# An attention, feed-forward and mixture-of-experts kernel on one core: the decay table is built through DRAM, and the first feed-forward units and the weight conversion move forward

## The chip, the cores and the metric

The kernel runs on one NeuronCore of a Trainium2 chip. The metric is device time in microseconds (us) of one execution. TensorE is called PE in the profile, VectorE DVE, ScalarE ACT, GpSimd POOL, and SyncE, which here only issues transfers, SP.

## The reference

Three layers follow one another on 1536 tokens of width 512. The first is linear attention with a decay per head, in blocks, with a running state per batch:

```
Dmask = where(rel >= 0, lam ** rel, 0)                       # per head
intra = ((q_block @ k_block.T) * Dmask) @ v_block
inter = (q_block * lam ** (pos + 1)) @ kv_state
out_block = intra + inter
kv_state = lam ** block * kv_state + (k_block * lam ** (block - 1 - pos)).T @ v_block
```

The second is a dense feed-forward layer, whose weights arrive as float64 bit patterns:

```
h = x @ w_in            # 512 x 2048
x = maximum(0.01 * h, h) @ w_out
```

The third picks one of eight experts per token by a gate and applies `relu(x @ w1[e]) @ w2[e]`, scaled by the gate.

## The kernel before

Each engine runs its instructions in the order in which the code writes them (a manual schedule); the order of the work is set by hand.

**Attention.** The 12 chunks of 128 tokens (`ORD`) are called 0 to 11. For a chunk, `at_scores` makes the scores on PE (tile `sc`), `at_mask` multiplies them on DVE by the decay table `dec` (tile `dec_t`, 128 x 8 heads x 128, result `pm`), `at_out` multiplies by `v` on PE (tile `ao`) and splits the result into a high and a low half for the next layer (`xh` on ACT, `xl` on DVE). `at_prep_q` multiplies queries by powers of the decay (`lq`, on POOL), `at_prep_k` the keys (on ACT for the chunks in `PREP_ACT`, else on POOL), `at_state` makes a chunk's contribution to the state on PE (tile `as`), and `at_state_add` puts it into the state (a copy on ACT for the first chunk of a batch, an addition on DVE after that). Chunks 0 and 1 are the first of the two batches.

**The decay table.** `make_dec` builds on DVE, in 8 rows of 256 numbers (`pw`, one row per head), zeros followed by the powers of lam. Line p of the table of head h is row h read from element p on. `load_dec` fetches it, before, by eight transfers out of `pw` in SBUF, one per head.

**Feed-forward.** Tokens are taken two chunks at a time (j = 0 to 5) and the hidden width in 16 slices f, so that there are 96 units u = 16 j + f. `ff1` makes 12 matmuls into `hp` and a scaled copy `t` on ACT, `ff1_max` the maximum on DVE, `ff1_split` the halves `gh` (ACT) and `gl` (DVE), and `ff2` six matmuls into `x`, `LAG` = 2 steps behind. The list `seq` gives the unit of each step i: 0, 1, 2, 16, 3, 17 and so on, so that from step 2 on each weight slice serves two units in turn. Attention work of later chunks hangs on the units as hooks (`at(j, f, ...)` runs behind unit 16 j + f).

**Weights.** Slice f has a tile `wi` and a tile `wo` (512 KB each as it arrives in `rawi`, `rawo`). Converting one takes four DVE instructions (three on bits at lines 1481 and 1486, one subtraction at line 1493) and one rounding on ACT (line 1491); `conv` does the same at lines 180 to 198 ahead of the loop. The table `todo` says which tiles a step converts: two in each of steps 0 to 2, one in each of steps 3 to 26. All loads go through SP's queue in the order of the code.

The lines to follow are `load_dec` (113), the mask (314), the split of the attention output (354, 355), the maximum (411) and the two lists at the end, `todo` and the hooks.

Of the kernel before, what the change touches and what calls it, by code (L numbers as in the profile page):

```python
# [18 lines left out]
B, H, S, D = 2, 8, 768, 64  # L19
NT, DM, DFF = 1536, 512, 2048  # L20
E, FE = 8, 1024
C = 128
# [4 lines left out]
NSTAT = 10  # L27
NPLAIN = 12
NAR = 32
PREP_ACT = (0, 1)  # L30
KV = {1: 'wo15', 2: 'wi15', 3: 'wo14'}
QK = {2: 'wi14', 3: 'wo13'}
NPOS = {2: 0, 3: 1, 4: 2}
# [7 lines left out]
def tile_attention_ffn_moe(  # L41
# [51 lines left out]
    def make_dec():  # L93
        nc.vector.memset(pw[:, 0:127], 0.0)
        nc.vector.memset(pw[:, 127:128], 1.0)
        nc.vector.tensor_copy(out=pw[:, 128:129], in_=lam_sb)
        m = 1
        while m < 128:
            nc.vector.tensor_scalar(
                out=pw[:, 128 + m:128 + 2 * m],  # L100
                in0=pw[:, 128:128 + m],
                scalar1=pw[:, 127 + m:128 + m],
                scalar2=None,
                op0=ALU.mult,
            )
            m *= 2

    def load_dec():

        base = pw[:, :]  # L110
        step = base.ap[0][0]
        for h in range(H):
            nc.sync.dma_start(
                out=dec[:, h, :],
                in_=bass.AP(tensor=base.tensor, offset=base.offset + h * step, ap=[[step, 1], [1, 128], [1, C]]),
            )

    def load_lq():
        nc.sync.dma_start(out=pw_d, in_=pw)
        base = pw_d[:, :]  # L120
        for half in range(2):
            nc.sync.dma_start(
                out=lq[half * 64:half * 64 + 64],
                in_=bass.AP(
                    tensor=base.tensor,
                    offset=base.offset + half * 256 + 128,
                    ap=[[0, 64], [512, H // 2], [1, C]],
                ),
            )
# [4 lines left out]
    def load_chunk(n, names):  # L134
        b, c = ORD[n]
        t = chunks.setdefault(n, {})
        for nm in names:
            if nm == "k" and c + 1 >= NCH:
                continue
            src = {"qT": qT, "kT": kT, "v": v, "k": k}[nm]  # L140
            if n in KV and nm in ("v", "k"):
                if "kv" not in t:
                    t["kv"] = wp.tile([128, 2, 512], F32, tag=KV[n], name="kv")
                t[nm] = t["kv"][:, int(nm == "k"), :]
            elif n in QK and nm in ("qT", "kT"):
                if "qk" not in t:
                    t["qk"] = wp.tile([128, 2, 512], F32, tag=QK[n], name="qk")
                t[nm] = t["qk"][:, int(nm == "kT"), :]
            else:
                t[nm] = qkv_p.tile([128, 512], F32, tag=nm, name=nm, bufs=2 if nm in ("qT", "kT") else 1)  # L150
            nc.sync.dma_start(out=t[nm], in_=src[b, c])
            if nm in ("qT", "kT"):
                t[nm] = t[nm].rearrange("p (g i) -> p g i", g=4)
            else:
                t[nm] = t[nm].rearrange("p (h d) -> p h d", h=H)
# [3 lines left out]
    def load_win(f):  # L159
        r = wp.tile([128, 4, 256], I32, tag=f"wi{f}", name=f"rawi{f}")  # L160
        nc.sync.dma_start(out=r.rearrange("p k f -> p (k f)"), in_=w_in[f])
        raw["wi", f] = r

    def load_wout(f):
        r = wp.tile([128, 1024], I32, tag=f"wo{f}", name=f"rawo{f}")
        nc.sync.dma_start(out=r, in_=w_out[f * 128:(f + 1) * 128, :])
        raw["wo", f] = r
# [93 lines left out]
    def warm_pe(n):  # L261
        wb = bank(0, "warm")
        for _ in range(n):
            nc.tensor.matmul(wb, lhsT=junk[:, 0:128], rhs=junk, start=True, stop=True)
# [9 lines left out]
    def at_prep_q(n):  # L274
        b, c = ORD[n]
        t = chunks[n]
        if c > 0:
            nc.gpsimd.tensor_mul(out=t["qT"], in0=t["qT"], in1=lq)  # L278
# [130 lines left out]
    def ff1_max(u):  # L409
        t, hp = gt[u]  # L410
        nc.vector.tensor_max(out=t, in0=t, in1=hp)  # L411
# [874 lines left out]
    def conv(tag, f, dst, eng):  # L1286
        split64_out(*split64([(tag, f, dst, eng)]))
# [2 lines left out]
    V, P = nc.vector, nc.gpsimd  # L1290
    nc.sync.dma_start(out=lam_sb, in_=lam.rearrange("(h o) -> h o", o=1))
    load_chunk(0, ("qT", "kT"))
    load_chunk(1, ("qT", "kT"))
    load_win(0)
    make_dec()
    load_dec()
    load_chunk(0, ("v",))
    load_chunk(1, ("v",))
    load_wout(0)
    load_chunk(0, ("k",))  # L1300
    load_chunk(1, ("k",))
    load_win(1)
    load_chunk(2, ("qT", "kT"))
    load_lq()
    load_chunk(3, ("qT", "kT"))
    load_wout(1)
    load_chunk(2, ("v", "k"))
    load_win(2)
    load_chunk(3, ("v", "k"))
    load_wout(2)  # L1310
    load_win(3)
    load_wout(3)
    load_win(4)
    load_wout(4)
    nc.scalar.copy(out=lam_sb2, in_=lam_sb)

    nc.gpsimd.memset(junk, 0.0)
    warm_pe(10)
    at_scores(0, 2, 7)
    conv("wi", 0, win, V)  # L1320
    at_scores(1, 5, 6)
    at_mask(0)
    at_mask_tw(1)
# [1 line left out]
    at_out(1, 4)  # L1325
    at_prep_k(0)
    at_prep_k(1)
    at_state(0, 2)
    at_state(1, 7)
    at_state_add(0)  # L1330
    at_state_add(1)
    conv("wo", 0, wout, V)

    NU = 16 * NCH
    last = NCH - 1
# [2 lines left out]
    def at(j, f, fn, *args):  # L1338
        hooks.setdefault(16 * j + f, []).append((fn, args))

    at(0, 0, at_out, 2, 2)
    at(0, 0, at_out, 3, 7)
    at(0, 1, at_state, 2, 3)
    at(0, 1, at_state, 3, 4)
    at(0, 1, at_state_add, 2)
    at(0, 1, at_state_add, 3)
    for f in range(11):
        at(0, f + 2, load_win, f + 5)
        at(0, f + 2, load_wout, f + 5)
# [112 lines left out]
            seq.append(16 + f - SKEW)  # L1462
    seq += range(32, NU)
    items = [(tag, f) for f in range(16) for tag in ("wi", "wo")]
    todo = {0: items[2:4], 1: items[4:6], 2: items[6:8]}
    for i in range(3, 27):
        todo[i] = items[i + 5:i + 6]
    late_sub = []

    def bits(job, n):  # L1470
# [21 lines left out]
        (win if tag == "wi" else wout)[f] = hl  # L1492
        late_sub.append(lambda: V.tensor_sub(out=hl[:, 1], in0=job[4].bitcast(F32), in1=hl[:, 0].bitcast(F32)))

    at_scores(2, 3, 4)
    at_prep_q(2)
    at_mask(2)
    at_scores(3, 5, 6)
    at_prep_q(3)
    at_mask(3)  # L1500
    at_prep_k(2)
    at_prep_k(3)
    for i in range(NU + LAG):
        u = seq[i] if i < NU else None
        if u is not None:
            ff1(u, i % 2)
            jobs = [[tag, f] for tag, f in todo.get(i, ())]
            for job in jobs:
                bits(job, 0)
            ff1_max(u)  # L1510
            for job in jobs:
                bits(job, 1)
            for fn in late_sub:
                fn()
            late_sub.clear()
            for job in jobs:
                bits(job, 2)
            ff1_split(u)
            for job in jobs:
                round_hi(job)  # L1520
            if i < 2:
                for fn in late_sub:
                    fn()
                late_sub.clear()
        if i >= LAG:
            w = seq[i - LAG]
            if w == NU - 1:
                G1(0, 0, 0, 7)
            ff2(w)
            if w % 16 == 15 and w // 16 not in (1, 2):  # L1530
                evac_x2(w // 16)
        for fn, args in hooks.get(u, ()):
            fn(*args)
# [156 lines left out]
```

## Time and profile before

| what | value |
|---|---|
| median of 3 runs | 546.64 us (545.68 to 546.86) |
| profiled execution | 545.67 us, its span in the trace 543.8 us |
| PE busy in the span | 498.4 us, 92% |
| DVE busy | 318.9 us, 59% |
| ACT busy | 174.4 us, 32% |
| POOL busy | 105.8 us, 19% |
| moved by DMA | 63.42 MB, mean 117 GB/s |

The profile follows one execution. The span is the time from the first to the last instruction of the trace; the 1.9 us between it and the execution's time lie around it. Times in rows count from the span's start. A busy share is a mean over stages that are limited by different things, so the stretch at the start is read by itself.

### The profile page before, as it was taken

How to read it: one execution, taken by the hardware profiler on the slowest of the kernel's cores; microseconds unless marked ns; L12 is line 12 of the kernel's file. 1: busy time of each engine (PE TensorE's matmuls, PEld its weight loads, DVE VectorE, ACT ScalarE, POOL GpSimd, SP SyncE). 2: the span in 40 equal slices, each digit the busy share in tenths (PEclk: the TensorE clock that was granted, in tenths of full speed). 3: DMA queues.
4: the chain of work that ended last, by engine and by line, in shares of the span. 5: the costliest groups of instructions: out<-in, count | busy, mean ns of one | idle time of the engine just before them, and what ended most of it. 6: DMA issues, size and time to landing. Idle time of an engine off the chain costs nothing. (4 is left out here: it accounts for less than half of the span.)

```text
span 543.8 us, 9414 instructions
## 1 busy us (share of the span) xinstructions
PE 498.4 (92%) x3488; PEld 424.1 (78%) x3488; DVE 318.9 (59%) x767; ACT 174.4 (32%) x409; POOL 105.8 (19%) x142
## 2 busy tenths in 40 slices
PE   4078799998999999999999999899999999999994
PEld 2067698787788888887898898787789997969693
DVE  3137989999867777768366737874652141613130
ACT  1052343333442223322232224544332253422221
POOL 1004001103202120102102106334031212232111
PEclk9577899999999999999999999999999999999998
DMA  6779950080090110310040007221049717365101
GB/s 131 91 250 410 401 209 1 0 288 1 9 303 4 40 41 0 108 41 29 0 156 2 21 1 235 75 61 57 4 137 382 265 39 264 131 200 196 40 2 41
DMA packets 30764, 63.42 MB, mean 117 GB/s; under 512 B 6967, under 2 KB 8895, under 8 KB 30704
## 3 DMA queue, kind: packets, MB, share of 16 engines
q1 hardware_dynamic: 28592, 56.17, 31.6%
q0 software_dynamic: 2112, 6.52, 3.5%
q8 instruction: 29, 0.48, 0.4%
q14 instruction: 31, 0.25, 0.1%
HBM read 55.83 MB, written 6.52 MB: 115 GB/s over the span
## 5 line engine op out<-in xcount | busy, mean ns | idle before, releaser
L403 PE MATMUL hp<-xh,wi 128*128 128x256 f32 x768 | 129.7, 292 | 8.9 <-ACT wi L1491 4.6
L403 PEld LDWEIGHTS hp<-xh,wi 128*128 128x128 f32 x768 | 110.6, 194 | 20.0 <-DVE t L411 6.3
L432 PE MATMUL x<-wo,gh 128*128 128x512 f32 x384 | 120.9, 396 | 0.0
L432 PE MATMUL x<-wo,gl 128*128 128x512 f32 x192 | 75.5, 393 | 2.2 <-DVE gl L419 2.2
L432 PEld LDWEIGHTS x<-wo,gh 128*128 128x128 f32 x384 | 66.5, 191 | 8.1
L418 ACT ACTIVATE gh<-t 128x256 fp32r<-128x256 f32 x96 | 40.1, 418 | 93.5 <-DVE t L411 93.5
L419 DVE TENSOR_TENSOR gl<-t,gh 128x256 fp32r<-128x256 f32 x96 | 45.2, 471 | 33.0 <-ACT gh L418 25.2
L403 PE MATMUL hp<-xl,wi 128*128 128x256 f32 x384 | 62.8, 287 | 0.0
L406 ACT ACTIVATE t<-hp 128x256 f32<-128x256 f32 x96 | 36.2, 377 | 72.7 <-PE hp L403 72.7
L962 PE MATMUL hp<-xp,w1h 128*128 128x256 f32 x320 | 58.7, 284 | 0.0
L411 DVE TENSOR_TENSOR t<-t,hp 128x256 f32<-128x256 f32 x96 | 40.0, 417 | 24.2 <-ACT t L406 22.6
L403 PEld LDWEIGHTS hp<-xl,wi 128*128 128x128 f32 x384 | 54.0, 195 | 0.0
L990 PE MATMUL o<-w2h,hp 128*128 128x512 f32 x160 | 52.5, 397 | 0.0
L962 PEld LDWEIGHTS hp<-xp,w1h 128*128 128x128 f32 x320 | 50.2, 192 | 2.6 <-issue 2.5
L972 DVE SCALAR_TENSOR_TENSOR hp<-hp,hp 128x256 fp32r<-128x256 f32 x40 | 16.5, 423 | 59.5 <-ACT hp L971 50.5
L432 PEld LDWEIGHTS x<-wo,gl 128*128 128x128 f32 x192 | 36.2, 189 | 13.3 <-DVE gl L419 5.6
L962 PE MATMUL hp<-xp,w1l 128*128 128x256 f32 x160 | 45.3, 283 | 0.0
L278 POOL TENSOR_TENSOR qT<-qT,lq 128x512 f32<-128x512 f32 x8 | 10.9, 1357 | 133.3 <-PE sc L301 107.3
L990 PEld LDWEIGHTS o<-w2h,hp 128*128 128x128 f32 x160 | 29.8, 188 | 7.0 <-issue 1.2
L990 PE MATMUL o<-w2l,hp 128*128 128x512 f32 x80 | 31.5, 394 | 0.0
L962 PEld LDWEIGHTS hp<-xp,w1l 128*128 128x128 f32 x160 | 30.7, 192 | 0.1
L513 DVE SCALAR_TENSOR_TENSOR junk<-x2s,wgr 128x512 bf16<-128x512 f32 x36 | 28.6, 796 | 0.6
(256 smaller groups left out, 659.6 us busy)
## 6 DMA issues: line engine op xcount, KB each, us to landing
rawi<-in_moe_w_in_dram SPq DMA_DIRECT2D x16, 512.0 KB, 8.1
rawo<-in_moe_w_out_dram SPq DMA_DIRECT2D x16, 512.0 KB, 8.3
raw<-in_moe_w_dram SPq DMA_DIRECT2D x16, 512.0 KB, 5.8
nr<-in_moe_w_dram SPq DMA_DIRECT2D x9, 512.0 KB, 6.1
xs_d<-x2s SPq DMA_DIRECT2D x12, 256.0 KB, 2.6
nrx<-in_moe_w_dram SPq DMA_DIRECT2D x6, 512.0 KB, 7.5
wgr_hi<-in_moe_w_dram SPq DMA_DIRECT2D x6, 512.0 KB, 9.0
qT<-in_q_dram SPq DMA_DIRECT2D x10, 256.0 KB, 4.4
```

The source lines that it names most:

```text
L278: nc.gpsimd.tensor_mul(out=t["qT"], in0=t["qT"], in1=lq)
L403: nc.tensor.matmul(hp, lhsT=w[:, hl, kk, :], rhs=xx[:, kk, :], start=(n == 0), stop=(n == 11))
L406: nc.scalar.activation(out=t, in_=hp, func=AF.Copy, scale=0.01)
L411: nc.vector.tensor_max(out=t, in0=t, in1=hp)
L418: nc.scalar.activation(out=gh, in_=t, func=AF.Copy)
L419: nc.vector.tensor_sub(out=gl, in0=t, in1=gh.bitcast(F32))
L432: nc.tensor.matmul(x2[j][tk], lhsT=a[:, ts], rhs=wout[f][:, w, :], start=(f == 0 and n == 0), stop=(f == 15 and n == 2),)
L513: nc.vector.scalar_tensor_tensor(out=junk, in0=xv, scalar=1.0, in1=wgr[e], op0=ALU.mult, op1=ALU.mult, accum_out=acc)
L962: nc.tensor.matmul(hp.rearrange("p (a b) -> p a b", a=2), lhsT=w1s[kk][w][:, f * 128:(f + 1) * 128], rhs=x[:, :, ks], start=(n == 0), stop ...
L972: nc.vector.scalar_tensor_tensor(out=lo, in0=hp, scalar=0.0, in1=hi.bitcast(F32), op0=ALU.max, op1=ALU.subtract)
L990: nc.tensor.matmul(o2[b], lhsT=hT[b, f // 4][a][fs], rhs=w[:, f % 2, :], start=(n == 0), stop=(n == 23))
```

## The change

The table's 8 rows go to DRAM first (`store_dec`), and `load_dec` reads the 128 x 8 lines of 512 bytes from there in two transfers of four heads each. Ahead of the table now stand only the load of lam, chunk 0's queries and keys, the first weight tiles `wi0` and `wo0`, and chunk 1's queries and keys. The state of chunks 0 and 1 and the scores of chunks 2 and 3 move from in front of the unit loop into hooks behind units 0 and 1; chunk 2's and 3's outputs and states move one step later each. `PREP_ACT` moves the key scaling of chunks 0 and 1 from ACT to POOL, and that of chunks 2 and 3 from POOL to ACT. Tiles `wi0`, `wo0` and `wi1` are converted ahead of the loop (before: `wi0` and `wo0`), so that the list in `todo` ends at step 25. In steps 0 to 2 the maximum stands ahead of the first bit instruction. The PE's warm-up has 7 matmuls where it had 10.

```diff
--- before.py
+++ after.py
@@ -27,7 +27,7 @@
 NSTAT = 10
 NPLAIN = 12
 NAR = 32
-PREP_ACT = (0, 1)
+PREP_ACT = (2, 3)
 KV = {1: 'wo15', 2: 'wi15', 3: 'wo14'}
 QK = {2: 'wi14', 3: 'wo13'}
 NPOS = {2: 0, 3: 1, 4: 2}
@@ -105,18 +105,21 @@
             )
             m *= 2
 
+    def store_dec():
+        nc.sync.dma_start(out=pw_d, in_=pw)
+
     def load_dec():
-
-        base = pw[:, :]
-        step = base.ap[0][0]
-        for h in range(H):
+        base = pw_d[:, :]
+        for i in range(2):
+            h = slice(i * H // 2, (i + 1) * H // 2)
             nc.sync.dma_start(
                 out=dec[:, h, :],
-                in_=bass.AP(tensor=base.tensor, offset=base.offset + h * step, ap=[[step, 1], [1, 128], [1, C]]),
+                in_=bass.AP(
+                    tensor=base.tensor, offset=base.offset + h.start * 256, ap=[[1, 128], [256, H // 2], [1, C]]
+                ),
             )
 
     def load_lq():
-        nc.sync.dma_start(out=pw_d, in_=pw)
         base = pw_d[:, :]
         for half in range(2):
             nc.sync.dma_start(
@@ -1290,34 +1293,36 @@
     V, P = nc.vector, nc.gpsimd
     nc.sync.dma_start(out=lam_sb, in_=lam.rearrange("(h o) -> h o", o=1))
     load_chunk(0, ("qT", "kT"))
-    load_chunk(1, ("qT", "kT"))
     load_win(0)
     make_dec()
+    store_dec()
+    load_wout(0)
+    load_chunk(1, ("qT", "kT"))
     load_dec()
     load_chunk(0, ("v",))
     load_chunk(1, ("v",))
-    load_wout(0)
+    load_win(1)
     load_chunk(0, ("k",))
     load_chunk(1, ("k",))
-    load_win(1)
+    load_lq()
     load_chunk(2, ("qT", "kT"))
-    load_lq()
+    load_wout(1)
+    load_win(2)
+    load_chunk(2, ("v", "k"))
     load_chunk(3, ("qT", "kT"))
-    load_wout(1)
-    load_chunk(2, ("v", "k"))
-    load_win(2)
-    load_chunk(3, ("v", "k"))
     load_wout(2)
     load_win(3)
+    load_chunk(3, ("v", "k"))
     load_wout(3)
     load_win(4)
     load_wout(4)
     nc.scalar.copy(out=lam_sb2, in_=lam_sb)
 
     nc.gpsimd.memset(junk, 0.0)
-    warm_pe(10)
+    warm_pe(7)
+    conv("wi", 0, win, V)
     at_scores(0, 2, 7)
-    conv("wi", 0, win, V)
+    conv("wo", 0, wout, V)
     at_scores(1, 5, 6)
     at_mask(0)
     at_mask_tw(1)
@@ -1325,11 +1330,7 @@
     at_out(1, 4)
     at_prep_k(0)
     at_prep_k(1)
-    at_state(0, 2)
-    at_state(1, 7)
-    at_state_add(0)
-    at_state_add(1)
-    conv("wo", 0, wout, V)
+    conv("wi", 1, win, V)
 
     NU = 16 * NCH
     last = NCH - 1
@@ -1338,12 +1339,24 @@
     def at(j, f, fn, *args):
         hooks.setdefault(16 * j + f, []).append((fn, args))
 
-    at(0, 0, at_out, 2, 2)
-    at(0, 0, at_out, 3, 7)
-    at(0, 1, at_state, 2, 3)
-    at(0, 1, at_state, 3, 4)
-    at(0, 1, at_state_add, 2)
-    at(0, 1, at_state_add, 3)
+    at(0, 0, at_state, 0, 2)
+    at(0, 0, at_state, 1, 7)
+    at(0, 0, at_state_add, 0)
+    at(0, 0, at_state_add, 1)
+    at(0, 0, at_scores, 2, 3, 4)
+    at(0, 0, at_prep_q, 2)
+    at(0, 0, at_mask, 2)
+    at(0, 1, at_scores, 3, 5, 6)
+    at(0, 1, at_prep_q, 3)
+    at(0, 1, at_out, 2, 2)
+    at(0, 1, at_mask, 3)
+    at(0, 1, at_prep_k, 2)
+    at(0, 2, at_state, 2, 3)
+    at(0, 2, at_out, 3, 7)
+    at(0, 2, at_prep_k, 3)
+    at(0, 2, at_state_add, 2)
+    at(1, 0, at_state, 3, 2)
+    at(0, 3, at_state_add, 3)
     for f in range(11):
         at(0, f + 2, load_win, f + 5)
         at(0, f + 2, load_wout, f + 5)
@@ -1462,9 +1475,9 @@
             seq.append(16 + f - SKEW)
     seq += range(32, NU)
     items = [(tag, f) for f in range(16) for tag in ("wi", "wo")]
-    todo = {0: items[2:4], 1: items[4:6], 2: items[6:8]}
-    for i in range(3, 27):
-        todo[i] = items[i + 5:i + 6]
+    todo = {0: items[3:5], 1: items[5:7], 2: items[7:9]}
+    for i in range(3, 26):
+        todo[i] = items[i + 6:i + 7]
     late_sub = []
 
     def bits(job, n):
@@ -1492,22 +1505,17 @@
         (win if tag == "wi" else wout)[f] = hl
         late_sub.append(lambda: V.tensor_sub(out=hl[:, 1], in0=job[4].bitcast(F32), in1=hl[:, 0].bitcast(F32)))
 
-    at_scores(2, 3, 4)
-    at_prep_q(2)
-    at_mask(2)
-    at_scores(3, 5, 6)
-    at_prep_q(3)
-    at_mask(3)
-    at_prep_k(2)
-    at_prep_k(3)
     for i in range(NU + LAG):
         u = seq[i] if i < NU else None
         if u is not None:
             ff1(u, i % 2)
             jobs = [[tag, f] for tag, f in todo.get(i, ())]
+            if i < 3:
+                ff1_max(u)
             for job in jobs:
                 bits(job, 0)
-            ff1_max(u)
+            if i >= 3:
+                ff1_max(u)
             for job in jobs:
                 bits(job, 1)
             for fn in late_sub:
```

SP's queue at the program's start, before (`pw` is the 8-row tile, `dec_t` the table, `rawi0` and `rawo0` the raw weights of slice 0, `kv` chunk 1's values and keys, `qk` queries and keys of chunk 2):

```order
L151 DMA qT_128<-in_q_dram 128x512
L151 DMA kT_130<-in_kt_dram 128x512
L151 DMA qT_132<-in_q_dram 128x512
L151 DMA kT_134<-in_kt_dram 128x512
L161 DMA rawi0_136<-in_moe_w_in_dram 128x1024
L113 DMA dec_t_97<-pw_94 128x1x128 x8
L151 DMA v_156<-in_v_dram 128x512
L151 DMA kv_158<-in_v_dram 128x512
L166 DMA rawo0_160<-in_moe_w_out_dram 128x1024
L151 DMA k_162<-in_k_dram 128x512
L151 DMA kv_158<-in_k_dram 128x512
L161 DMA rawi1_165<-in_moe_w_in_dram 128x1024
```

and with the change:

```order
L154 DMA qT_128<-in_q_dram 128x512
L154 DMA kT_130<-in_kt_dram 128x512
L164 DMA rawi0_132<-in_moe_w_in_dram 128x1024
L109 DMA pw_d_92<-pw_94 8x256
L169 DMA rawo0_145<-in_moe_w_out_dram 128x1024
L154 DMA qT_147<-in_q_dram 128x512
L154 DMA kT_149<-in_kt_dram 128x512
L115 DMA dec_t_97<-pw_d_92 128x4x128 x2
L154 DMA v_153<-in_v_dram 128x512
L154 DMA kv_155<-in_v_dram 128x512
L164 DMA rawi1_157<-in_moe_w_in_dram 128x1024
L154 DMA k_159<-in_k_dram 128x512
```

The eight table loads become one store and two loads; the raw tile `rawo0` moves ahead of the table, chunk 1's queries and keys behind the first weight tile.

DVE's queue behind the mask of chunks 0 and 1, before (`xl` is the low half of the attention output, `wo0` the converted tile, `hp0` unit 0's first product):

```order
L355 TENSOR_TENSOR xl_254<-ao3_244,xh_253 128x4x128
L355 TENSOR_TENSOR xl_254<-ao4_257,xh_253 128x4x128
L180 TENSOR_SCALAR tw_306<-rawo0_160 128x512
L184 SCALAR_TENSOR_TENSOR tw_306<-rawo0_160,tw_306 128x512
L188 SCALAR_TENSOR_TENSOR tw_306<-rawo0_160,tw_306 128x512
L198 TENSOR_TENSOR wo0_310<-tw_306,wo0_310 128x512
L314 TENSOR_TENSOR pm_324<-sc3_313,dec_t_97 128x512
L314 TENSOR_TENSOR pm_326<-sc4_314,dec_t_97 128x512
L314 TENSOR_TENSOR pm_339<-sc5_328,dec_t_97 128x512
L314 TENSOR_TENSOR pm_341<-sc6_329,dec_t_97 128x512
L1481 TENSOR_SCALAR tw_360<-rawi1_165 128x512
L1481 TENSOR_SCALAR tw_362<-rawo1_176 128x512
```

and with the change, from the same two instructions on:

```order
L358 TENSOR_TENSOR xl_252<-ao3_242,xh_251 128x4x128
L358 TENSOR_TENSOR xl_252<-ao4_255,xh_251 128x4x128
L183 TENSOR_SCALAR tw_268<-rawi1_157 128x512
L187 SCALAR_TENSOR_TENSOR tw_268<-rawi1_157,tw_268 128x512
L191 SCALAR_TENSOR_TENSOR tw_268<-rawi1_157,tw_268 128x512
L201 TENSOR_TENSOR wi1_272<-tw_268,wi1_272 128x512
L414 TENSOR_TENSOR t_288<-t_288,hp0_275 128x256
L1494 TENSOR_SCALAR tw_291<-rawo1_167 128x512
L1494 TENSOR_SCALAR tw_293<-rawi2_169 128x512
L1499 SCALAR_TENSOR_TENSOR tw_291<-rawo1_167,tw_291 128x512
L1499 SCALAR_TENSOR_TENSOR tw_293<-rawi2_169,tw_293 128x512
L1499 SCALAR_TENSOR_TENSOR tw_291<-rawo1_167,tw_291 128x512
```

Between the split of the attention output and unit 0's maximum stood the conversion of `wo0`, two masks and two bit instructions; now the conversion of `wi1` stands there alone. On PE, unit 0's 12 matmuls now follow the outputs of chunks 0 and 1 directly; before, two states and two chunks of scores came first.

## Rows read from the trace of the kernel before

**Rows 1.** The page: the span, and PE's busy time.

```profile
span 543.8 us, 9414 instructions
...
PE 498.4 (92%) x3488; PEld 424.1 (78%) x3488; DVE 318.9 (59%) x767; ACT 174.4 (32%) x409; POOL 105.8 (19%) x142
```

**Rows 2.** Who waited for whom in 0 to 60 us: total, times, longest.

```profile
PE ao L330 <- DMA v<-in_v_dram: 17.6, 1, 17.6
...
DVE pm L314 <- PE ao L330: 6.4, 1, 6.4
```

**Rows 3.** Timeline of SP's queue, 0 to 40 us: start, duration, transfer.

```profile
4.10 14.58 SPq L113 DMA_DIRECT2D dec_t<-pw  x8
...
27.25 0.57 SPq L119 DMA_DIRECT2D pw_d<-pw  x1
...
33.57 1.61 SPq L122 DMA_DIRECT2D lq<-pw_d  x2
```

**Rows 4.** DMA issues of 0 to 60 us: count, KB each, median us to landing.

```profile
dec_t<-pw SPq DMA_DIRECT2D x8, 64.0 KB, 10.2
...
lq<-pw_d SPq DMA_DIRECT2D x2, 128.0 KB, 3.0
```

**Rows 5.** Stretches: busy time of each engine, granted PE clock, DMA share, GB/s.

```profile
0.00:6.00 6.00, 3.72 (x9) 1.31 (x10) 1.86 (x10) 1.47 (x2) 1.68 (x8) 1.00 0.60 173
...
9.00:10.00 1.00, 0.00 (x0) 0.00 (x0) 0.97 (x2) 0.00 (x0) 0.00 (x0) 1.00 0.66 25
...
36.00:37.00 1.00, 0.87 (x10) 0.57 (x6) 0.55 (x1) 0.42 (x1) 0.00 (x0) 0.56 0.78 133
...
44.00:60.00 16.00, 11.35 (x103) 10.17 (x100) 15.18 (x28) 4.73 (x11) 4.36 (x5) 0.81 1.03 410
...
51.00:52.00 1.00, 1.00 (x6) 1.00 (x6) 1.00 (x3) 1.00 (x3) 0.00 (x0) 0.50 1.02 406
```

**Rows 6.** Timeline of DVE, 0 to 66 us: start, duration, instruction, idle time before.

```profile
2.32 1.75 DVE L99 TENSOR_SCALAR pw<-pw 8x1 f32<-8x1 f32 x7
...
8.27 0.43 DVE L180 TENSOR_SCALAR tw<-rawi 128x512 int32<-128x512 int32 x1 [4.20 <-DMA rawi<-in_moe_w_in_dram]
...
10.84 0.69 DVE L198 TENSOR_TENSOR wi<-tw,wi 128x512 fp32r<-128x512 f32 x1 [0.70 <-ACT wi L197]
...
24.87 2.48 DVE L314 TENSOR_TENSOR pm<-sc,dec_t 128x512 f32<-128x512 f32 x4 [13.33 <-DMA v<-in_v_dram]
...
30.55 0.69 DVE L355 TENSOR_TENSOR xl<-ao,xh 128x512 fp32r<-128x512 f32 x1 [1.01 <-ACT xh L354]
...
44.73 1.29 DVE L314 TENSOR_TENSOR pm<-sc,dec_t 128x512 f32<-128x512 f32 x2 [6.39 <-PE ao L330]
...
48.74 1.10 DVE L1486 SCALAR_TENSOR_TENSOR tw<-rawi,tw 128x512 int32<-128x512 int32 x1
...
53.53 0.41 DVE L1481 TENSOR_SCALAR tw<-rawi 128x512 int32<-128x512 int32 x1
...
58.48 1.76 DVE L389 TENSOR_TENSOR st<-st,as 64x256 f32<-64x256 f32 x4
...
60.27 0.43 DVE L1481 TENSOR_SCALAR tw<-rawi 128x512 int32<-128x512 int32 x1
...
64.86 0.42 DVE L411 TENSOR_TENSOR t<-t,hp 128x256 f32<-128x256 f32 x1 [0.30 <-ACT t L406]
```

**Rows 7.** Timeline of DVE, 66 to 80 us, two successive maxima.

```profile
71.86 0.42 DVE L411 TENSOR_TENSOR t<-t,hp 128x256 f32<-128x256 f32 x1 [0.30 <-ACT t L406]
...
75.06 0.42 DVE L411 TENSOR_TENSOR t<-t,hp 128x256 f32<-128x256 f32 x1 [0.30 <-ACT t L406]
```

**Rows 8.** Timeline of ACT, 24 to 80 us: one chunk's key scaling.

```profile
30.42 2.01 ACT L287 ACTIVATE k<-k,dec_t 128x64 f32<-128x64 f32 x8
```

**Rows 9.** Timeline of PE, 0 to 80 us.

```profile
57.13 1.05 PE L403 MATMUL hp<-xh,wi 128*128 128x256 f32 x4 [2.34 <-ACT wi L1491]
...
74.15 0.64 PE L403 MATMUL hp<-xh,wi 128*128 128x256 f32 x4
...
76.97 0.64 PE L403 MATMUL hp<-xh,wi 128*128 128x256 f32 x4
```

## The prediction

> **What bounds the kernel now.** The page comes first: PE is busy 498.4 of 543.8 us [rows 1], so the kernel as a whole is a PE kernel and only stretches in which PE stands still can give anything. The chain that ended last covers only the final scatter, so I went to the waits of the first 60 us instead. One wait rules there: PE waits 17.6 us before the output of chunk 0, and what it waits for is put down to the load of `v` [rows 2]. The reader should not stop at that name. SP's queue shows why `v` is late: the eight transfers of the table hold the queue from 4.10 us for 14.58 us [rows 3], each needs 10.2 us to land [rows 4], and while they run the DMA engines show a busy share of 0.66 yet move 25 GB/s [rows 5]. Everything behind them (`v`, `rawo0`, `k`, `rawi1`, chunk 2) starts that late. The first mask runs at 24.87 us [rows 6].
>
> Next, what is limited after that. From the second mask pair at 44.73 us on, DVE runs without a gap to 64 us, and in the loop one maximum follows the next every 3.20 us (71.86 to 75.06) with 0.30 us of waiting for ACT in it [rows 6, 7]. A PE step in the same stretch takes 2.82 us (74.15 to 76.97) [rows 9]. So while weights are converted, the DVE and ACT loop sets the pace and not PE; PE only eats up a lead. What counts is therefore when DVE reaches step 3, the maximum at 64.86 us [rows 6], and a shift there should pass through to the end, since what follows hangs on program order.
>
> **The table's time.** `pw` is done at 2.32 + 1.75 = 4.07 us [rows 6]. The store is then issued at 4.1. Its landing has an upper bound in the same store of before, 6.3 us from issue (27.25) to the load that needs it (33.57) [rows 3], with a full queue ahead; the lower bound is nothing. I take 3.0 us, what the small `lq` loads need in a queue that is nearly empty [rows 4], as only chunk 0 and `wi0` (1.05 MB) stand ahead here, and the first 6 us moved 173 GB/s or 1.04 MB [rows 5]: landed at 7.1. The two table loads are like the two `lq` loads, from the same 8 KB in DRAM in lines of 512 bytes, and twice their bytes. Those two took about 3.9 us together (1.61 us of issue, 0.9 of it for the first by estimate, and 3.0 us for the second) [rows 3, 4], in which 133 GB/s was seen in their main microsecond [rows 5]. The other 0.26 MB at 133 GB/s add 2.0 us: landed at 13.0. The far bound is the old rate: 0.52 MB at 25 GB/s is 21 us, landed at 28. I take 13.0, as `lq` shares source, line length and queue with the new loads, while the old loads share only line length and the one-number step from line to line.
>
> DVE has work before that: two conversions of 3.26 us each (8.27 to 10.84 + 0.69) [rows 6]. `rawi0` now has 1.05 MB to wait for and not 1.57, so about 6.3 us; 6.3 + 6.5 = 12.8. The first mask then stands at 13.0, where it stood at 24.87: **11.9 us**.
>
> [...]
>
> **From the first mask to step 3.** Call the first mask M. Before, M to the second `xl` is 24.87 to 31.24: 6.4 us [rows 6], and I keep it. Then: conversion of `wi1` 3.3, done at M + 9.6. Unit 0's matmuls run meanwhile on PE, as they no longer wait for chunk 2's loads. Step 0 without disturbance costs what step 1 cost before: 53.53 to 58.48, 4.95 us [rows 6]: M + 14.6. Chunk 2's mask pair 1.3 (as 44.73) [rows 6]: M + 15.9. Step 1, 4.95: M + 20.9. Chunk 2's split 0.7 and chunk 3's mask 1.3: M + 22.9. Step 2 without its two subtractions, 60.27 to 64.15 (which is 64.86 less the 0.42 and the 0.30 of wait that lead up to it), 3.9 [rows 6, 7]: M + 26.8. Then DVE waits for ACT, which has roundings and chunk 3's high half in front: 1.0 by estimate; split 0.7 and state addition 0.9 (half of 1.76) [rows 6]: M + 29.4. Bits and maximum of step 3, 1.0: M + 30.4.
>
> Three costs on top. POOL: step 0 of before took 53.53 - 45.94 less two splits of 0.6, or 6.4 us where 4.95 is the clean price; bit instructions were drawn out to 1.10 us [rows 6] while POOL was busy (4.36 us in 44 to 60) [rows 5]. POOL's scalings of chunks 2 and 3 and its state work meet the bits again: 1.5 us. The key scaling on ACT: one chunk costs 2.01 us [rows 8], now for chunks 2 and 3 right before the copies `t` of steps 2 and 3; the first hides behind the split and mask of DVE, the second mostly behind the state addition: 0.5 us, with 4.0 as the bound if neither hides. [...] The three fewer warm-up matmuls I cost at nothing, since PE then waits for chunk 1's keys in either case; if not hidden, the scores of chunk 1 take 1 us more, still ahead of the mask.
>
> Sum: step 3's maximum at 13.0 + 30.4 + 2.6 = 46.0 us, where it was 64.86: 18.9 us earlier. Not all stays: chunk 3's state addition now comes at step 4 and costs DVE 0.9, and the conversion ends a step earlier, which turns one step of 3.20 into one of 2.82: 0.4 gained [rows 6, 7, 9]. **18.4 us.** The loads don't catch up with that: at 410 GB/s [rows 5] a slice of 1.05 MB takes 2.6 us, and two steps use it in 6.4. The SP queue keeps its order from slice 5 on, so what later waits for chunk 4 and 5 keeps its place.
>
> 545.67 - 18.4 = 527.3 for the profiled execution; the median of the runs is 1.0 above that one, so **528**.
>
> **Rivals.** (1) The forecast, 524 to 533: chance 0.70. (2) PE and ACT become the bound of the first three steps, because in these the maximum stands ahead of the bits and DVE stands still until matmuls and copy are done. Each unit at the low clock is 2.9 us plus 0.4 for the copy; were 2 us of it open in each step, 18.4 becomes about 12: 534 (532 to 538). For it speaks the 2.3 us gap already seen in front of a unit [rows 9]; against it, that weights are converted one tile ahead, so no unit waits for its own conversion. Chance 0.15. (3) The table from DRAM comes no faster than from SBUF, its lines costing what they cost before. Then M is 28.1, step 3 at 61.1, and of the change remain 3.3 us: 543. Against it stands `lq`. Chance 0.07. [...] (4) Slower: all 1024 lines come from one 8 KB piece of DRAM, and if they queue for it, the load can be slower than the old one. It decides at M = 31.4 us, that is 24 us for the two loads, or 22 GB/s; at half the old rate M is 49 and the time 564. For it: `lq` had only 512 lines and eight starting points. Chance 0.03. (5) The gain is made but given back in the loop, because PE arrives there without the lead that it had before (it ran at 2.82 against 3.20 for some eight steps): 540 or so, 0.03. Better than 524, because PE's gaps at the start vanish altogether: 0.02.
>
> **How the numbers follow.** 528 is the likeliest case. From 523.5 to 536.5 lie nearly all of (1) and most of (2), about 0.82. A measurement of this kernel can tell some 0.2%, 1.1 us, from no change. Faster by more: (1), (2), (5), the better case and most of (3), 0.94; within it: the end of (3), 0.02; slower: (4) and a stray of (3), 0.04.
>
> **What would show it.** Right: both table loads landed by 12 to 15 us at above 100 GB/s, the first mask at 13 to 14, DVE without a gap over 2 us from there to step 3, step 3's maximum near 46, and the same 3.2 us from maximum to maximum afterwards. Wrong: a wait of the mask for the table beyond 16 us (3, 4); gaps on DVE ending with ACT's copy `t` in steps 0 to 3 (2); or a step 3 at 46 and yet less gain at the end (5).

## The result and the profile after

The change takes 525.25 us (median of 4 runs, 524.47 to 525.76) where the kernel before takes 546.16 us on the same chip (545.58 to 546.86): a ratio of 0.9615, with a 95% interval of 0.9596 to 0.9634. That is 20.9 us less, 2.75 us better than the forecast of 528 and inside its range. The profiled execution took 525.76 us. Its page:

```profile
span 523.7 us, 9395 instructions
...
PE 493.7 (94%) x3485; PEld 420.6 (80%) x3485; DVE 319.6 (61%) x767; ACT 174.1 (33%) x409; POOL 105.7 (20%) x142
```

Against [rows 1] the span is 20.1 us shorter and PE's busy time 4.7 us: three quarters of the gain, 15.4 us, is time in which PE stood still, and 1.1 us of the rest are the three warm-up matmuls (ten took 4.24 us, seven take 3.17). SP's queue shows where it began (start, duration, transfer):

```profile
4.09 0.30 SPq L109 DMA_DIRECT2D pw_d<-pw  x1
...
7.22 0.93 SPq L115 DMA_DIRECT2D dec_t<-pw_d  x2
8.20 0.50 SPq L154 DMA_DIRECT2D v<-in_v_dram  x1
```

The queue is held by the table for 0.93 us and not for 14.58 [rows 3], and `v` is issued at 8.20 us. The landing time (count, KB each, median us) and three stretches of the windows view (busy time of PE, PEld, DVE, ACT, POOL, granted PE clock, DMA share, GB/s):

```profile
dec_t<-pw_d SPq DMA_DIRECT2D x2, 256.0 KB, 4.9
```

```profile
9.00:10.00 1.00, 0.00 (x0) 0.00 (x0) 0.45 (x1) 0.51 (x1) 0.00 (x0) 1.00 0.67 213
...
28.00:34.00 6.00, 3.84 (x22) 3.25 (x23) 6.00 (x13) 2.19 (x6) 0.00 (x0) 0.50 1.02 407
...
44.00:60.00 16.00, 16.00 (x113) 14.15 (x112) 14.47 (x31) 6.09 (x14) 0.00 (x0) 1.00 0.80 310
```

In the microsecond from 9 to 10 the DMA engines have the same busy share as before, 0.67 against 0.66 [rows 5], and move 213 GB/s where they moved 25. From 44 to 60 us PE now has no idle time at all; before it was busy 11.35 of these 16 us [rows 5]. DVE's timeline, which the prediction followed (idle time before an instruction and what ended it in brackets):

```profile
6.97 0.43 DVE L183 TENSOR_SCALAR tw<-rawi 128x512 int32<-128x512 int32 x1 [2.91 <-DMA rawi<-in_moe_w_in_dram]
...
12.72 0.69 DVE L201 TENSOR_TENSOR wo<-tw,wo 128x512 fp32r<-128x512 f32 x1 [0.69 <-ACT wo L200]
13.33 2.48 DVE L317 TENSOR_TENSOR pm<-sc,dec_t 128x512 f32<-128x512 f32 x4
17.30 0.69 DVE L358 TENSOR_TENSOR xl<-ao,xh 128x512 fp32r<-128x512 f32 x1 [1.49 <-ACT xh L357]
18.47 0.69 DVE L358 TENSOR_TENSOR xl<-ao,xh 128x512 fp32r<-128x512 f32 x1 [0.48 <-ACT xh L357]
...
22.26 0.41 DVE L414 TENSOR_TENSOR t<-t,hp 128x256 f32<-128x256 f32 x1
...
22.92 1.52 DVE L1494 TENSOR_SCALAR tw<-rawi 128x512 int32<-128x512 int32 x1
...
26.77 1.48 DVE L422 TENSOR_TENSOR gl<-t,gh 128x256 fp32r<-128x256 f32 x1
...
29.38 1.28 DVE L317 TENSOR_TENSOR pm<-sc,dec_t 128x512 f32<-128x512 f32 x2
30.57 0.41 DVE L414 TENSOR_TENSOR t<-t,hp 128x256 f32<-128x256 f32 x1
...
35.52 0.69 DVE L358 TENSOR_TENSOR xl<-ao,xh 128x512 fp32r<-128x512 f32 x1
...
37.42 0.42 DVE L414 TENSOR_TENSOR t<-t,hp 128x256 f32<-128x256 f32 x1
...
40.83 0.42 DVE L422 TENSOR_TENSOR gl<-t,gh 128x256 fp32r<-128x256 f32 x1
42.10 0.69 DVE L358 TENSOR_TENSOR xl<-ao,xh 128x512 fp32r<-128x512 f32 x1 [0.84 <-ACT xh L357]
42.71 0.86 DVE L392 TENSOR_TENSOR st<-st,as 64x256 f32<-64x256 f32 x2
...
44.57 0.42 DVE L414 TENSOR_TENSOR t<-t,hp 128x256 f32<-128x256 f32 x1 [0.55 <-ACT t L409]
...
48.37 0.42 DVE L414 TENSOR_TENSOR t<-t,hp 128x256 f32<-128x256 f32 x1 [0.29 <-ACT t L409]
...
52.20 0.42 DVE L414 TENSOR_TENSOR t<-t,hp 128x256 f32<-128x256 f32 x1
55.40 0.42 DVE L414 TENSOR_TENSOR t<-t,hp 128x256 f32<-128x256 f32 x1 [0.30 <-ACT t L409]
58.59 0.42 DVE L414 TENSOR_TENSOR t<-t,hp 128x256 f32<-128x256 f32 x1 [0.30 <-ACT t L409]
```

Two times matter. The first mask runs at 13.33 us, 11.5 us earlier than in [rows 6], right behind the conversion of `wo0` and with no wait for the table. (The mask reads the scores and the table, not `v`, so the wait of 13.33 us that [rows 6] puts down to `v` must have been one for the table.) The maximum of step 3 stands at 44.57 us, 20.3 us earlier. Between the two no wait on DVE exceeds 1.5 us, and the maxima of steps 0 to 2 wait for nothing. Behind step 3 the pace is what it was, 3.20 us (55.40 to 58.59). From step 3's maximum to the end of the span it is 479.1 us (523.7 - 44.57), and before it was 478.9 (543.8 - 64.86): what is won by step 3 stays won.

### The profile page after: what moved, and what is told of

Same layout as the page of the kernel before. It is cut to its first block, busy times and chain, and to the rows that moved or that the text cites. A ratio compares the mean times of both kernels' runs of the same rounds, so it can differ in the third digit from the quotient of the medians.

```text
span 523.7 us, 9395 instructions
## 1 busy us (share of the span) xinstructions
PE 493.7 (94%) x3485; PEld 420.6 (80%) x3485; DVE 319.6 (61%) x767; ACT 174.1 (33%) x409; POOL 105.7 (20%) x142
## 5 line engine op out<-in xcount | busy, mean ns | idle before, releaser
L406 PE MATMUL hp<-xh,wi 128*128 128x256 f32 x768 | 127.4, 288 | 4.4 <-DVE t L414 2.7
L406 PEld LDWEIGHTS hp<-xh,wi 128*128 128x128 f32 x768 | 109.4, 192 | 13.2 <-DVE t L414 4.9
L422 DVE TENSOR_TENSOR gl<-t,gh 128x256 fp32r<-128x256 f32 x96 | 46.3, 482 | 33.4 <-ACT gh L421 26.1
```

The costliest lines, as they stand in the source:

```text
L406: nc.tensor.matmul(hp, lhsT=w[:, hl, kk, :], rhs=xx[:, kk, :], start=(n == 0), stop=(n == 11))
L422: nc.vector.tensor_sub(out=gl, in0=t, in1=gh.bitcast(F32))
```

## The experiments

Theory A is the prediction's: what counts is when DVE, with ACT, arrives at step 3, and the table and the order of the start each bring a part of that. The rivals are named where a run tells them apart. Their step-3 times and spans stand together behind the last run.

**The table alone.** The kernel before, with the store and the two loads from DRAM in place of the eight transfers, all else where it was:

```diff
     def load_dec():
-        base = pw[:, :]
-        for h in range(H):
+        nc.sync.dma_start(out=pw_d, in_=pw)
+        base = pw_d[:, :]
+        for i in range(2):
...
```

> The kernel before, with only the table's path changed: one store of the 8 rows to DRAM and two loads of four heads each, at the place in the queue where the eight transfers stood. Theory A (DVE's way to step 3 decides; table and order each give a part): the table lands near 13.3 us, the first mask with it, and the old order then needs some 36 us to step 3's maximum where it needed 40, because its loads are no longer late; step 3 near 49.6, time 531 (529 to 534). Theory B (the late table was the only thing wrong, the new order gives nothing by itself): 525 to 527. Theory C (the order alone moves the units, the table's path gives its 11.5 us at the mask and the rest is lost to later waits): 535 or more.

Measured: 529.75 us (529.5 to 530.43), ratio 0.9703 (0.9689 to 0.9717). DVE's timeline:

```profile
12.82 2.48 DVE L315 TENSOR_TENSOR pm<-sc,dec_t 128x512 f32<-128x512 f32 x4 [1.77 <-DMA dec_t<-pw_d]
...
48.04 0.42 DVE L412 TENSOR_TENSOR t<-t,hp 128x256 f32<-128x256 f32 x1 [0.30 <-ACT t L407]
```

Here the mask waits for the table itself, so the landing can be read: 12.8 us. From there to step 3 it is 35.2 us (some 36 expected), and the time lies in theory A's range; B and C are out. The table brings four fifths of the gain; 4.5 us are left for the order.

**The order alone.** The change, with the eight transfers out of SBUF where the two loads stand:

```diff
-        base = pw_d[:, :]
-        for i in range(2):
+        base = pw[:, :]
...
+        for h in range(H):
...
```

> The changed kernel, with only the table's path put back to eight transfers out of SBUF (the store to DRAM stays, for the lq loads). Theory A: the table lands near 27 us, the mask with it, and DVE needs the same 31.2 us from there to step 3: maximum near 58.5, time 539 (537 to 541), so still faster than before by some 7. Theory B: as before within 1 us, 546. Theory C: 532 or less.

Measured: 542.38 us (539.97 to 544.07), ratio 0.994 (0.9922 to 0.9959); the profiled execution is the fastest of these, with a span of 538.1:

```profile
26.64 2.48 DVE L315 TENSOR_TENSOR pm<-sc,dec_t 128x512 f32<-128x512 f32 x4 [13.58 <-DMA v<-in_v_dram]
...
58.61 0.42 DVE L412 TENSOR_TENSOR t<-t,hp 128x256 f32<-128x256 f32 x1 [0.56 <-ACT t L407]
```

The step-3 time is the expected one, 6.3 us ahead of before, although the first mask is 1.8 us later; the profiled gain is 5.7 us of span, that of the medians 3.9. The median lies outside the 537 to 541 us of theory A: the forecast of step 3 held, that of the time did not. Why the other executions were up to 4 us slower than the profiled one no trace shows. By the medians the two parts nearly add up: 0.9703 x 0.994 is 0.9645, and both together give 0.9615. At step 3 they overlap: 16.8 and 6.3 us apart, 20.3 together. With the late table the order takes 8.0 us off the way from the first mask to step 3 (40.0 before, 32.0 here), with the early table 4.0 (35.2 and 31.24).

**Without the tile ahead.** The change with `wi1` converted in step 0, as before:

```diff
-    conv("wi", 1, win, V)
...
-    todo = {0: items[3:5], 1: items[5:7], 2: items[7:9]}
-    for i in range(3, 26):
-        todo[i] = items[i + 6:i + 7]
+    todo = {0: items[2:4], 1: items[4:6], 2: items[6:8]}
+    for i in range(3, 27):
+        todo[i] = items[i + 5:i + 6]
```

> The changed kernel without the conversion one tile further ahead: wi1 is converted in step 0 again, and the conversions end at step 26. Theory A (the loop is paced by DVE and ACT, so each tile converted ahead costs its full 3.3 us in front and saves only 0.4 of a loop step): step 3 comes 1 to 3 us earlier, one more loop step at 3.2 instead of 2.8, in all 523.5 (522.5 to 525), slightly faster than the change. Theory D (the tile ahead keeps units 1 and 2 from waiting for their own weights, and that is part of the gain): PE and then DVE wait 1 to 2 us in each of steps 0 to 2, 527 to 529.

Measured: 526.98 us over 6 runs that lie far apart (524.62 to 529.44), ratio 0.9652 (0.9629 to 0.9676). Its profile has step 3's maximum at 44.81 us, 0.24 behind the change's. So theory A's forecast failed: step 3 was to come 1 to 3 us earlier, but in place of converting DVE waits 1.73 and 0.76 us for the copies `t` of steps 0 and 1. It was run again beside the change:

> The change itself once more, beside the two other kernels of this call on one chip, as their measure. Every theory: 525.3 us (524.4 to 526).

> The kernel without the tile ahead once more, since its runs were far apart (524.6 to 529.4) and its profile had step 3's maximum at 44.81 us, within 0.3 us of the change's. Theory D, the tile ahead is part of the gain: 527 to 528, at least 1.5 us over the change on the same chip, and the step-3 maximum at 46 or later. Rival A, it only moves waits about (DVE waits 1.7 and 0.8 us for the copies t in place of converting): 525.5 to 526.3, within 1 us of the change.

Measured: the change 526.32 us (525.72 to 528.93), ratio 0.9633 (0.9611 to 0.9655); without the tile ahead 528.75 (526.74 to 530.05), ratio 0.9647 (0.9627 to 0.9668). The change itself came out above its expected 524.4 to 526 us; the kernel before took 547.03 us on this chip, 0.9 more than beside the first result. The medians stand as D expected and the intervals overlap, and the change had one execution of 528.93 us too. But this time the profile caught the slowest of the five executions (530.05 us), and it shows what happens in it. DVE's timeline, PE's, and two windows of it:

```profile
30.34 1.50 DVE L1493 TENSOR_SCALAR tw<-rawi 128x512 int32<-128x512 int32 x1
...
45.71 0.69 DVE L358 TENSOR_TENSOR xl<-ao,xh 128x512 fp32r<-128x512 f32 x1 [3.08 <-ACT xh L357]
...
48.19 0.42 DVE L414 TENSOR_TENSOR t<-t,hp 128x256 f32<-128x256 f32 x1 [0.56 <-ACT t L409]
```

```profile
35.55 0.74 PE L406 MATMUL hp<-xh,wi 128*128 128x256 f32 x4 [3.23 <-ACT wi L1503]
...
42.06 1.89 PE L333 MATMUL ao<-pm,kv 128*64 128x128 f32 x16
```

```profile
34.00:36.00 2.00, 0.45 (x3) 0.45 (x4) 2.00 (x4) 1.13 (x2) 0.29 (x1) 1.00 1.04 414
...
40.00:42.00 2.00, 2.00 (x19) 1.25 (x20) 2.00 (x4) 0.28 (x1) 0.00 (x0) 0.50 1.02 408
```

Unit 2 waits 3.23 us for its own tile `wi`, whose bits took longer than usual while POOL was busy: one 1.50 us where 0.42 is usual, with POOL busy for 1.27 us from 30 to 32. In the first profile one of them was drawn out too (1.75 us where 0.68 is usual, POOL busy for 1.34 us from 30 to 32), but there PE came to unit 2 later and waited 0.51 us. Behind that gap the granted clock is 0.50 while chunk 3's output is computed; that takes 1.89 us where the first profile of this kernel has 1.05, and DVE waits 3.08 us for the high half `xh` in place of 0.85. Step 3 is 3.4 us later than in the first profile, 2.2 of it from this wait and 0.9 from a later first mask (13.69 and 12.82), and the end 3.7. So the tile ahead gives nothing in the good case, and it takes away a wait that can grow. D fits such an execution; by the medians it stays unsettled.

**The key scaling swapped back** to ACT for chunks 0 and 1 and POOL for 2 and 3:

```diff
-PREP_ACT = (2, 3)
+PREP_ACT = (0, 1)
```

> The changed kernel with the key scaling put back: chunks 0 and 1 on ACT, 2 and 3 on POOL. Theory A: the two scalings (2.0 us each) stand on ACT between the splits and the rounding of wi1 and unit 0's copy, so DVE waits some 3 us at wi1 and unit 0, and POOL's scalings meet two more of DVE's bit instructions, 1 us each: 529 (527 to 531). Rival (the scalings are hidden wherever they stand): 525 within 1 us.

Measured: 528.19 us (527.76 to 528.91), ratio 0.9666 (0.965 to 0.9682). DVE's timeline:

```profile
22.75 0.69 DVE L201 TENSOR_TENSOR wi<-tw,wi 128x512 fp32r<-128x512 f32 x1 [1.86 <-ACT wi L200]
...
46.55 0.42 DVE L414 TENSOR_TENSOR t<-t,hp 128x256 f32<-128x256 f32 x1 [0.55 <-ACT t L409]
```

DVE waits 1.86 us for ACT's rounding of `wi1`, behind the key scaling there, and three of its bit instructions in step 0 take 1.52 to 1.74 us, where 0.42 and 0.68 are usual, beside three POOL instructions of 1.30 to 1.50 us. The swap is thus worth some 2.0 us at step 3, and the rival is out. The prediction had given it no gain of its own.

**The maximum behind the first bits** in steps 0 to 2, as in before:

```diff
-            if i < 3:
-                ff1_max(u)
...
-            if i >= 3:
-                ff1_max(u)
+            ff1_max(u)
```

> The change with the maximum behind the first bit instructions in steps 0 to 2, as it stands in before. Theory A, DVE's way to step 3 decides and no maximum there waits for ACT: the order of instructions that run without a gap changes nothing, step 3's maximum at 44.6 (44.2 to 45.2) and 525.5 us (524.5 to 526.5). Rival E, PE's lead in the first steps matters: the second products of units 0 to 2 come 0.7 us later each, step 3 at 46 to 47, and 527 to 528.

Measured: 526.69 us (526.25 to 527.5), ratio 0.9627 (0.9611 to 0.9642), step 3's maximum at 44.93; the change on the same chip has 0.9633. Step 3 came as A said; the time is 0.2 us above A's range, on the chip on which the change took 526.32. The change, its repeat and the kernel with the later rounding (below) have the same code up to step 3 and differ by 0.8 us there (44.48 to 45.31), so these runs can tell no difference: where DVE runs without gaps, the place of one instruction among the others is worth nothing that shows.

**Is it the start addresses?** The lines of a head start one number apart. In two kernels all lines of a head start at the same place, 128 numbers into its row, once from SBUF in the kernel before and once from DRAM in the change. The table's values are then not the reference's, and only the transfer's time is read.

```diff
...
-  offset=base.offset + h * step, ap=[[step, 1], [1, 128], [1, C]]
+  offset=base.offset + h * step + 128, ap=[[step, 1], [0, 128], [1, C]]
...
```

```diff
...
-  offset=base.offset + h.start * 256, ap=[[1, 128], [256, H // 2], [1, C]]
+  offset=base.offset + h.start * 256 + 128, ap=[[0, 128], [256, H // 2], [1, C]]
...
```

> The kernel before, with every line of a head's table read from the same start in its SBUF row instead of one number further on each, so that the values of the table are not the reference's: only the time of the eight transfers is read. If the source (one SBUF row for all 128 lines) makes them slow: the same 25 GB/s, first mask near 24.9 us. If the shifting, unaligned starts do: far above 25 GB/s and the mask before 16 us.

> The changed kernel, with every line of a head's table read from the same start in DRAM, so that the values of the table are not the reference's: only the time of the two loads is read. They took 4.9 us to land. [...]

One window and the landing from SBUF, and then the landing from DRAM:

```profile
9.00:10.00 1.00, 0.00 (x0) 0.00 (x0) 0.95 (x2) 0.00 (x0) 0.00 (x0) 1.00 0.70 27
```

```profile
dec_t<-pw SPq DMA_DIRECT2D x8, 64.0 KB, 6.9
```

```profile
dec_t<-pw_d SPq DMA_DIRECT2D x2, 256.0 KB, 6.6
```

From SBUF the rate is 27 GB/s where it was 25 [rows 5], SP's queue is held for 13.42 us where it was 14.58 [rows 3], and the first mask comes at 23.39 us, 1.5 earlier: the starts are a small part of what made it slow. What the large part is stays open, since no run separates the source (one SBUF row, or DRAM) from the form (eight transfers of 128 lines, or two of 512). From DRAM the landing took 6.6 us and not 4.9. But the same loads with shifted starts took 4.0 us with the table alone and 5.7 with the bits earlier (below), so that one execution shows no more than that the lines with one start did not come sooner. The whole kernels took 544.19 and 527.57 us in single runs.

**Is it DVE with ACT that sets the pace of the loop?** In the change, from step 3 on, ACT's rounding of a tile is put behind the next step's copy `t`, so that the maximum doesn't wait for it:

```diff
+            for job in late_round:
+                round_hi(job)
+            late_round.clear()
...
-            for job in jobs:
-                round_hi(job)
+            if i < 3:
+                for job in jobs:
+                    round_hi(job)
+            else:
+                late_round += jobs
```

> The changed kernel, with the rounding of a tile that is converted in the loop (from step 3 on) moved on ACT behind the next step's copy t, so that DVE's maximum no longer waits 0.30 us for ACT in each step. Theory A (DVE and ACT pace steps 3 to 25): a step goes from 3.20 to about 2.90 us, 22 steps, some 6 us less: 519 (518 to 521). Theory E (PE paces these steps and DVE's waits are only its slack): no change, 525 within 1 us.

Measured: 521.07 us (520.39 to 521.3), ratio 0.9536 (0.9522 to 0.9549), span 519.2. DVE's timeline, and ACT's:

```profile
58.40 0.41 DVE L414 TENSOR_TENSOR t<-t,hp 128x256 f32<-128x256 f32 x1
61.21 0.41 DVE L414 TENSOR_TENSOR t<-t,hp 128x256 f32<-128x256 f32 x1
```

```profile
59.80 0.39 ACT L409 ACTIVATE t<-hp 128x256 f32<-128x256 f32 x1 [0.55 <-PE hp L406]
```

The wait of 0.30 us is gone, a step takes 2.81 us and not 3.20, and now the copy `t` waits for PE: the loop has come down to PE's 2.82 [rows 9], where it stops. The gain is 4.2 us, the time 0.1 above A's range, and E is out; behind step 3 the span is 5.2 us shorter. This kernel is faster than the one before and the change.

**Bits earlier on top of that.** The bits of `wo0` ahead of the subtraction of `wi0`, those of `wi1` ahead of the split of chunks 0 and 1, so that DVE doesn't wait for ACT there:

```diff
-    conv("wi", 0, win, V)
+    first = [split64([("wi", 0, win, V)]), split64([("wo", 0, wout, V)])]
...
-    conv("wo", 0, wout, V)
+    for x in first:
+        split64_out(*x)
...
+    second = split64([("wi", 1, win, V)])
...
-    conv("wi", 1, win, V)
+    split64_out(*second)
```

> The kernel with the later rounding (521.07 us measured), and on DVE the bits of wo0 ahead of the subtraction of wi0 and the bits of wi1 ahead of the split of chunks 0 and 1, so that the waits for ACT there (0.7 three times, 1.5 and 0.5 before the splits) are filled. Theory A, carried on: the first mask 0.6 us earlier (then the table's landing near 12.6 bounds it), 2 us less between the splits and unit 0's maximum, of which one is lost to waiting for rawo1: 519 (518 to 520.5). Rival (from step 3 on PE alone sets the pace there now, and it can't start earlier because its inputs come from ACT in the same order): 521 within 0.7.

Measured: 520.4 us (519.59 to 521.72), ratio 0.9529 (0.9509 to 0.9549), which can't be told from the kernel without it and lies in both theories' ranges. The first mask comes at 12.37 us and waits 1.16 us for the table there; afterwards DVE waits 1.12 us for the copy `t` of step 0 and 0.63 us for `rawi2`. The waits went elsewhere.

**Together.** First mask, step 3's maximum, and the span less the latter, in us from the profiled executions:

| kernel | first mask | step 3 | span - step 3 |
|---|---|---|---|
| before | 24.87 | 64.86 | 478.9 |
| the change | 13.33 | 44.57 | 479.1 |
| the change again | 12.57 | 44.48 | 479.3 |
| table alone | 12.82 | 48.04 | 479.6 |
| order alone | 26.64 | 58.61 | 479.5 |
| without the tile ahead | 12.82 | 44.81 | 479.5 |
| the same again | 13.69 | 48.19 | 479.8 |
| key scaling swapped back | 13.16 | 46.55 | 479.6 |
| maximum behind the bits | 13.26 | 44.93 | 479.6 |
| rounding late in the loop | 13.41 | 45.31 | 473.9 |
| bits earlier on top | 12.37 | 43.69 | 474.0 |

In the nine executions with the loop of before, step 3 moves over 20 us and the rest stays within 0.9. Only the two with a faster loop have another rest.

## Why the prediction was right

**What bounds the kernel** held: a shift of step 3's maximum passes through to within 0.9 us, in all nine rows of the table above. The prediction took 0.5 us off it (0.9 for the later state addition, 0.4 back); the span lost 0.2 of 20.3. Chunk 3's addition moved into step 4 as foreseen (three steps later than before, not one as the list of the changes has it), and 48.37 to 52.20 is 3.83 us where 3.20 is usual, so 0.6. The earlier end of the conversion pays all of it back. Behind it, the same unit's maximum stands, before and after, at

```profile
158.06 0.42 DVE L411 TENSOR_TENSOR t<-t,hp 128x256 f32<-128x256 f32 x1 [0.89 <-ACT t L406]
```

```profile
137.77 0.42 DVE L414 TENSOR_TENSOR t<-t,hp 128x256 f32<-128x256 f32 x1 [0.88 <-ACT t L409]
```

which is 20.29 us apart, as at step 3.

**The size.** 528 was 2.75 us too high. Between the profiled executions, which the sum was made for, 527.3 stands against 525.76, so the kernel accounts for 1.5 of it. The rest is where these executions lie among the runs: the forecast put the median above the profiled one, and it came 0.5 us below. At step 3 the sum was 1.4 us late (46.0 and 44.57): the first mask came 0.3 us later than forecast, the way from it took 1.8 us less. These errors, and those within the way, partly cancel, which is luck.

**The table's time** held. The loads were issued at 7.22 us (7.1 predicted); in three runs whose mask waits for them they landed at 12.4 to 12.8, and at 13.7 in a fourth (13.0 predicted). The repeat of the change, SP's queue and DVE:

```profile
6.21 0.93 SPq L115 DMA_DIRECT2D dec_t<-pw_d  x2
```

```profile
12.57 2.48 DVE L317 TENSOR_TENSOR pm<-sc,dec_t 128x512 f32<-128x512 f32 x4 [0.19 <-DMA dec_t<-pw_d]
```

The rate that the prediction asked for, above 100 GB/s, did not hold as stated: from the first issue to the mask it took 4.9 us with nothing but the table's path changed, 6.25 with the bits earlier and 6.36 in the repeat, which for 0.52 MB is 107, 84 and 82 GB/s for the table by estimate, so above 100 in the first of them only. In the other two `rawo0` and chunk 1's queries and keys stand right ahead of it in the queue; from 9 to 10 us the engines of the change's first profile moved 213 GB/s in all. The mask of that first profile hangs on DVE's two conversions instead (6.97 us plus two of 3.2), which the prediction had 0.2 us ahead of the table because it put the landing of `rawi0` at 6.3; that the mask still stood within 0.3 us of the forecast is in part luck. The bound it feared, the old rate, is out, and with it rivals (3) and (4).

The lines have 512 bytes before and after. Out of SBUF, in eight transfers, they moved at 25 GB/s with shifted starts and 27 with one start (9 to 10 us); out of DRAM, in two, at 82 to 107 GB/s by estimate.

**From the first mask to step 3** the forecast was 33.0 us and the trace has 31.24. By its own terms:

| term | predicted | measured |
|---|---|---|
| mask to the end of the second `xl` | 6.4 | 5.8 |
| conversion of `wi1` | 3.3 | 3.1 |
| step 0, undisturbed | 4.95 | 4.95 |
| POOL's collisions | 1.5 | 2.2 |
| chunk 2's mask | 1.3 | 1.2 |
| step 1 | 4.95 | 4.95 |
| split and chunk 3's mask | 2.0 | 1.9 |
| step 2 | 3.9 | 3.8 |
| wait for ACT | 1.0 | 0.85 |
| split and state addition | 1.6 | 1.5 |
| bits and maximum of step 3 | 1.0 | 1.0 |
| key scaling on ACT | 0.5 | 0 |
| PE's clock | 0.6 | 0 |

Four terms were off by half a microsecond or more. The second `xl` waited 0.48 us for ACT and not 1.01 [rows 6], which makes most of the first; in the kernel with the maximum behind the bits, whose code is the same up to there, it waited 1.01 again, so this part is chance of the execution. Two DVE instructions beside POOL's scalings of the queries took 1.52 and 1.48 us where 0.42 is the clean price: 2.2 us, the whole of what step 0 took above 4.95. POOL's timeline names the scalings, `lq` being the factor:

```profile
22.73 1.42 POOL L281 TENSOR_TENSOR qk<-qk,lq 128x512 f32<-128x512 f32 x1 [4.32 <-PE sc L304]
26.52 1.45 POOL L281 TENSOR_TENSOR qk<-qk,lq 128x512 f32<-128x512 f32 x1 [2.37 <-PE sc L304]
```

Each of the two DVE instructions (22.92 to 24.44 us and 26.77 to 28.25) starts 0.2 us behind one on POOL and ends about 0.3 us behind its end (24.15 and 27.97).

The key scaling cost nothing. It ends at 43.98 us (41.97 and 2.01, on ACT), and the copy `t` behind it still waited 0.18 us for PE:

```profile
41.97 2.01 ACT L290 ACTIVATE kv<-kv,dec_t 128x64 f32<-128x64 f32 x8
44.16 0.39 ACT L409 ACTIVATE t<-hp 128x256 f32<-128x256 f32 x1 [0.18 <-PE hp L406]
```

No run shows the 0.6 us that stand in the sum for PE's clock (with 1.5 and 0.5 they make its 2.6); in its place the change's trace has a low clock that is hidden. Ahead of chunk 2's output PE waits 3.76 us, and the granted clock is 0.50 from 28 to 34 us:

```profile
30.16 2.52 PE L333 MATMUL ao<-pm,kv 128*64 128x128 f32 x16 [3.76 <-ACT t L409]
```

DVE is busy 6.00 of these 6 us, above all with step 1's bits, and doesn't need that output earlier. The repeat without the tile ahead shows the price where the cover is gone: 2.2 us more of waiting.

**Rivals.** (2) fails: no maximum of steps 0 to 2 waits for matmul or copy, and putting it later changes nothing that shows. (Its 2.9 us for a unit at the low clock are what unit 0's 12 matmuls took before, from 50.56 to 53.48 us, where the granted clock was 0.50 from 51 to 53.) (5) fails: the loop goes on at 3.20 us, and the rest of the span is as long as before (479.1 and 478.9). The order's share, which the prediction did not price apart, is 4.0 us of the way from the first mask to step 3 (35.2 with the table alone, 31.24 with both), and about half of that is the swap of the key scaling (33.4 us without it).

## What to carry to other kernels

When a wait is put down to a load, look at what stands ahead of that load in its queue, and compare bytes moved with the busy share of the DMA engines: 25 GB/s at 0.66 was the sign of transfers that are slow in themselves: the same engines moved 410 GB/s at 1.03 [rows 5]. Then find the point from which the rest of the program runs at its own fixed pace and price a change of the start as the shift of that point; here that held within 0.9 us over 20. And once the start is cheap, look at that pace: moving one rounding on ACT gave another 4 us.

## What the runs showed of the hardware that was not expected

- Lines of 512 bytes out of one SBUF row at a time came at 25 GB/s with shifted starts and at 27 with the same start, from 9 to 10 us.
- The same two table loads out of DRAM took 4.0 us to land with the table alone, 4.9 in the change and 5.7 with the bits earlier; with all lines of a head read from one place it was 6.6 us in the one execution there is.
- A stretch of low granted clock (0.50) moves between executions of one kernel: in the two profiles without the tile ahead it lies at 26 to 30 us in one and at 38 to 42 us in the other. In the first DVE then waited 0.76 us for a copy `t`, in the second 3.08 us for `xh` (0.85 in the first).
